# RWKV attention with a Fourier-mixing MLP block: six input tiles and four sets of chunk tiles in place of seven and three, with a new stored order

## The chip, the cores and the metric

The kernel runs on one core of a Trainium2 chip. The core has a matrix engine (PE, whose weight loads PEld overlap its matmuls), a vector engine (DVE), a scalar engine (ACT), GpSimd (POOL) and a queue engine (SP) that here only starts transfers between the chip's main memory (HBM) and the on-chip memory (SBUF). PE writes to eight banks of a second memory, PSUM. The metric is the device time of one execution in microseconds (us).

## The reference

Attention is a recurrence over 768 steps for 4 batches and 8 heads of 48 columns, with r, k, v and w of shape (4, 8, 768, 48) and u of shape (8, 48); its output, with the heads side by side, is x of shape (4, 768, 384). Behind it stand a two-dimensional Fourier transform of which the real part is kept, a layer norm, and an MLP with 1536 hidden columns:

```
def _attn_ref(r, k, v, w, u):
...
    for t in range(S):
...
        cur = np.einsum('bhd,bhe->bhde', u[None] * kt, vt)
        y[:, :, t] = np.einsum('bhd,bhde->bhe', rt, state + cur)
        state = wt[:, :, :, None] * state + np.einsum('bhd,bhe->bhde', kt, vt)
    return y.astype(np.float32)

def _moe_ref(x, w_ch1, w_ch2):
    X = np.fft.fft(x, axis=1)
    X = np.fft.fft(X, axis=2)
    mixed = np.real(X).astype(np.float32)
    u = x + mixed
...
    un = (u - mu) / np.sqrt(var + 1e-06)
    ch = np.maximum(un @ w_ch1, 0.0) @ w_ch2
    return (u + ch).astype(np.float32)
```

## The kernel before

**Attention in chunks.** Each batch is cut into six chunks of 128 steps, n = 0 to 23 in all. A chunk's four inputs (w, k, r, v, each 128 steps by 384 columns, fp32, 192 KB) are loaded by `load_one` (line 624) into one of NIN = 7 tiles of each kind, number n mod 7. `attention` (from line 783) takes the logarithm of w (LB, line 797), sums it over the steps on PE with a triangular mask (799, and 822 for the sum from the other side), and takes exponentials: those for r in place in PSUM or in the tile of w (852, 859), those for k in E2 with the chunk's whole decay (826, 836 to 840). RH is r times the first, KH is k times E2; the two stand side by side in RKH. Both are transposed into RKT, either by PE with a copy out of PSUM (893 to 911; the copies show at line 601 on ACT and 602 on DVE), or from batch 1 on by one DMA started by SP (889). The scores of KT and RT (922) are masked into AH (932 on DVE; or copied by ACT at 937 and masked in SBUF). The term with u is a dot product for each head: RK = r k, then RK times UB (u spread over all partitions, 660), then a sum over the head (DC, 871), and VTD = v DC. The state ST is carried from chunk to chunk (956, 959, 967), y is ST with RT plus AH with VB (984, 987; VB is v in bf16), and X = y + VTD (998). E2, RK, DC, AH and LB have NB = 3 tiles, number n mod 3; RKH and RKT have NT = 4. PE's sum for chunk n waits until the masks of chunk n - 2 are done.

**Mixing and MLP.** When chunks c and c + 3 of a batch are there, `fold` makes sums and differences of them (SD, XF). `mix` (from line 1048) does both transforms as matmuls (1063 to 1068, HCS, HCR, 1107), adds x (UF), normalises (UN), transposes in two halves of three tiles of 128 rows (UNT: by PE at 1203, or by a DMA of SP at 1210), multiplies by W1 (1235; HT is the rectified result, evicted by DVE at 1241 or by ACT at 1243) and W2 (1254), and evicts with the residual (OSB, 1263), which SP stores (1274). Elementwise work on SBUF tiles that either DVE or POOL can do shows at the helper lines 578 to 602. POOL's queue also starts the three loads of the weights (769, 774). PE does 32 filler matmuls (1321) that nothing reads.

**What sets the order.** All this is written down as numbered operations: `op` records one, and `choose` records several ways to do a step. The table `ORDER` lists for each engine the numbers in the order in which it runs them; a way whose numbers aren't in the table isn't taken. `schedule` only derives the PSUM banks from it by a model of times, and lets an operation of POOL on two SBUF tiles wait for the last such operation of DVE that the model puts ahead of it. `emit` gives each engine its list with the waits that the data need. An engine never overtakes within its list; SP, too, issues its transfers in the order of its list.

Of the kernel before, what the change touches and what calls it, by code (L numbers as in the profile page):

```python
# [7 lines left out]
ALU = mybir.AluOpType  # L8
# [442 lines left out]
def bass_rwkv6_finch__then__fnet_fourier_mix_kernel(  # L451
# [27 lines left out]
    def sb(name, shape, dt):  # L479
        return nc.alloc_sbuf_tensor(name, [128] + list(shape), dt).ap()  # L480

    NIN = 7
    NB = 3
    NT = 4
    INB = {n: [sb("in_%s%d" % (n, i), [H, D], FP32) for i in range(NIN)] for n in "wkrv"}
# [869 lines left out]
```

## Time and profile before

| what | us |
|---|---|
| median of 3 runs (lowest, highest) | 182.34 (182.21, 183.43) |
| the profiled execution: its own time | 182.32 |
| the profiled execution: its span | 180.2 |
| PE busy | 172.6 (96%) |
| DVE busy | 155.7 (86%) |
| ACT busy | 130.2 (72%) |
| POOL busy | 111.0 (62%) |

The span is what the profiler shows from the first to the last instruction; the rest of the execution's time lies around it. Matmuls are pipelined and their ends are modelled, so a busy PE is not PE at its peak. The granted clock of PE is at full speed in all slices. The 16 DMA engines together move 29.29 MB. Where the trace says that an engine waited "<- DMA in_w", the load of w into the tile ended the wait; "SPq" is an issue on SP's queue, and its length is the time that the issue held up the queue.

### The profile page before, as it was taken

The numbers are of one execution on the slowest core, as the hardware profiler recorded it, in microseconds if no ns is written. First come the engines' busy times: TensorE is split into PE (matmuls) and PEld (weight loads), VectorE is DVE, ScalarE is ACT, GpSimd is POOL, SyncE is SP. The second block draws the span as 40 slices with busy tenths as digits, with TensorE's granted clock in tenths as the row PEclk, the third lists the DMA queues.
The fourth block names the chain that finished last, engine by engine and source line by source line (L and its number), as shares of the span: only waits on it lengthen the run. The fifth ranks groups of instructions, "written<-read, shape, count | busy, mean of one in ns | idle before, by whom it ended". The sixth has DMA issues, their size and how long they took to land.

```text
span 180.2 us, 4569 instructions
## 1 busy us (share of the span) xinstructions
PE 172.6 (96%) x1704; PEld 113.9 (63%) x1704; DVE 155.7 (86%) x372; ACT 130.2 (72%) x311; POOL 111.0 (62%) x140
## 2 busy tenths in 40 slices
PE   5988899999999999999999999999999999999994
PEld 2455566766666576866676766665666776656663
DVE  7699999779998899999999999799999966882543
ACT  3989979589899686899997994986981754290500
POOL 2437779697464588599899865898988070310000
PEclk9999999999999999999999999999999999999999
DMA  5999998998998989999899999999973213304113
GB/s 118 209 209 204 178 200 169 183 208 163 171 206 173 211 166 241 202 204 210 191 216 187 232 161 210 233 160 196 217 162 51 91 44 63 135 4 100 39 58 131
DMA packets 117303, 29.29 MB, mean 163 GB/s; under 512 B 112545, under 2 KB 117282, under 8 KB 117282
## 3 DMA queue, kind: packets, MB, share of 16 engines
q1 hardware_dynamic: 115698, 26.65, 73.5%
q0 software_dynamic: 1584, 2.36, 7.7%
q8 instruction: 13, 0.21, 0.5%
q14 instruction: 8, 0.07, 0.1%
HBM read 23.59 MB, written 4.72 MB: 157 GB/s over the span
## 4 chain that ended last, share of the span: by engine, by line
PE 78%; DVE 7%; DMA 5%; ACT 4%; SPq 2%; issue 2%; POOL 1%; DVEq 0%; POOLq 0%; ACTq 0%
PE bank L1254 23%; PE bank L1235 23%; PE bank L1107 4%; PE bank L922 3%; PE bank L1063 3%; DMA in_v<-in_v_dram 3%; PE bank L911 3%; PE bank L1321 2%; PE bank L987 2%; DMA in_w<-in_w_dram 2%; PE bank L799 2%; PE bank L984 2%; PE bank L959 2%; SPq L889 1%; DVE ah L932 1%
## 5 line engine op out<-in xcount | busy, mean ns | idle before, releaser
L1254 PE MATMUL bank<-w,ht 128*128 128x384 bf16 (+2 forms) x300 | 52.8, 319 | 0.0
L1235 PE MATMUL bank<-unt,w 128*128 128x384 bf16 x288 | 52.0, 326 | 0.0
L1243 ACT ACTIVATE ht<-bank 128x384 bf16<-128x384 f32 x70 | 31.2, 497 | 13.2 <-PE bank L1235 13.0
L1254 PEld LDWEIGHTS bank<-w,ht 128*128 128x128 bf16 x300 | 27.5, 98 | 15.4
L1235 PEld LDWEIGHTS bank<-unt,w 128*128 128x128 bf16 x288 | 27.0, 98 | 15.7 <-DVE ah L932 0.2
L932 DVE TENSOR_TENSOR ah<-bank,msk 128x512 bf16<-128x512 f32 x42 | 27.4, 682 | 0.2 <-PE bank L922 0.2
L578 POOL TENSOR_TENSOR rkh<-in_k,e 128x384 bf16<-128x384 f32 x19 | 19.0, 1002 | 7.2 <-ACT e L840 4.9
L1263 DVE SCALAR_TENSOR_TENSOR osb<-bank,rstd,uf 128x384 f32<-128x384 f32 (+2 forms) x25 | 14.7, 596 | 9.0 <-PE bank L1254 9.0
L578 POOL TENSOR_TENSOR vtd<-in_v,dc 128x384 f32<-128x384 f32 x22 | 18.1, 830 | 5.7 <-DVE rk L578 4.1
L578 POOL TENSOR_TENSOR rk<-in_r,in_k 128x384 f32<-128x384 f32 x18 | 17.9, 1001 | 0.0
L578 POOL TENSOR_TENSOR rk<-rk,ub 128x384 f32<-128x384 f32 x17 | 16.9, 997 | 0.8 <-DVE rk L578 0.5
L1241 DVE TENSOR_SCALAR ht<-bank 128x384 bf16<-128x384 f32 x26 | 13.7, 547 | 2.9 <-PE bank L1235 2.9
L601 ACT ACTIVATE rkt<-bank 128x512 bf16<-128x512 bf16 (+1 forms) x19 | 14.5, 781 | 1.1 <-PE bank L911 1.1
L592 ACT ACTIVATE lb<-in_w 128x384 bf16<-128x384 f32 x24 | 12.3, 521 | 3.0 <-DMA in_w<-in_w_dram 2.9
L592 ACT ACTIVATE vb<-in_v 128x384 bf16<-128x384 f32 x23 | 11.9, 522 | 2.2 <-DMA in_v<-in_v_dram 2.2
L578 POOL TENSOR_TENSOR xf<-sd 128x384 bf16<-128x384 f32 (+1 forms) x9 | 8.9, 999 | 7.4 <-DVE xf L578 5.0
L871 DVE TENSOR_REDUCE dc<-rk 128x8 f32<-128x384 f32 (+1 forms) x24 | 12.5, 526 | 0.1
L853 DVE TENSOR_TENSOR rkh<-bank,in_r 128x384 bf16<-128x384 f32 x21 | 11.5, 547 | 0.4 <-ACT bank L852 0.4
L998 DVE TENSOR_TENSOR x<-bank,vtd 128x384 f32<-128x384 f32 x21 | 11.4, 549 | 0.2 <-POOL vtd L578 0.2
L826 ACT ACTIVATE e<-bank 128x392 f32<-128x392 f32 (+1 forms) x18 | 8.8, 497 | 3.4 <-PE bank L813 2.6
L852 ACT ACTIVATE bank<-bank 128x384 f32<-128x384 f32 x21 | 10.1, 486 | 1.7 <-PE bank L799 1.6
L987 PE MATMUL bank<-vb,ah 128*128 128x48 bf16 x192 | 11.1, 183 | 0.0
(185 smaller groups left out, 373.2 us busy)
## 6 DMA issues: line engine op xcount, KB each, us to landing
in_w<-in_w_dram SPq DMA_DIRECT2D x24, 192.0 KB, 3.8
in_r<-in_r_dram SPq DMA_DIRECT2D x24, 192.0 KB, 3.8
in_k<-in_k_dram SPq DMA_DIRECT2D x24, 192.0 KB, 3.9
in_v<-in_v_dram SPq DMA_DIRECT2D x24, 192.0 KB, 4.0
out_dram<-osb SPq DMA_DIRECT2D x23, 192.0 KB, 2.8
w<-in_moe_w_ch_dram POOLq DMA_DIRECT2D x2, 576.0 KB, 8.6
w<-in_moe_w_ch_dram POOLq DMA_DIRECT2D x1, 1152.0 KB, 11.1
out_dram<-osb SPq DMA_DIRECT2D x1, 128.0 KB, 1.7
```

Source lines behind the costliest of these rows:

```text
L578: return lambda e: e.tensor_tensor(out=o, in0=a, in1=b, op=f)
L592: return lambda e: e.activation(o, a, f, **kw)
L601: {"act": lambda e: e.activation(o(), i(), ACTF.Copy), "dve": lambda e: e.tensor_copy(out=o(), in_=i())}, **kw)
L853: op("dve", v_1(DM), lambda e: e.tensor_tensor(out=rh[:, :, 0:D], in0=ps(tce)[:, 0:DM].rearrange("t (h d) -> t h d", d=D), in1=rt[:, :, :] ...
L871: op("dve", v_1(H * m), lambda e: e.tensor_reduce(out=dc[:, :], in_=rku[:, :, 0:m], axis=mybir.AxisListType.X, op=ALU.add), r=[("RK", i2)] ...
L932: masked[n].append(op("dve", v_1(512), lambda e: e.tensor_tensor(out=ah[:, x:H:2, :], in0=ps(bk)[:, :].rearrange("p (h t) -> p h t", t=128 ...
L987: ins = e.matmul(ps(ty)[:, D * h:D * h + D], ah[:, h, :], vb[:, h, :], start=first and not ype, stop=True, skip_group_check=True)
L1235: ins = e.matmul(ps(t)[:, 0:384], W1[:, m, 256 * (j // 2) + j % 2:256 * (j // 2) + 256:2], unt[:, :, m, :], start=(m == 0), stop=(m == NM ...
L1241: {"dve": lambda e, j=j, t=t, ht=ht: e.tensor_scalar(out=ht[:, j, :], in0=ps(t)[:, 0:384], scalar1=su, scalar2=0.0, op0=ALU.mult, op1=ALU. ...
L1243: "act": lambda e, j=j, t=t, ht=ht: e.activation(ht[:, j, :], ps(t)[:, 0:384], ACTF.Relu, scale=su)},
L1254: ins = e.matmul(ps(t)[:, 0:hi - lo], ht[:, j, 128 * x:128 * x + 128], W2[:, j, lo:hi], start=(j == 0), stop=(j == NJ - 1))
L1263: op("dve", v_1(hi - lo) + 64, lambda e: e.scalar_tensor_tensor(out=o[:, lo:hi], in0=ps(t)[:, 0:hi - lo], scalar=rstd[:, kb:kb + 1], in1=u ...
```

## The change

The input tiles go from seven to six of each kind, and E2, RK, DC and AH from three to four; LB stays at three. The product RK times UB moves from the common path into the way `dots`. A further way `dots_pe` is written for batch 0, which would do the dot product on PE; the new table doesn't take it. What it needs is made all the same in `bonus`: a pattern HV by POOL, UBD from it by two instructions of DVE, three small fp32 matmuls on PE (`spread`) and one product of DVE; nothing reads the result. And the table `ORDER` is new as a whole.

```
-    NIN = 7
-    NB = 3
+    NIN = 6
+    NB = 4
     NT = 4
...
-    LB = [sb("lb%d" % i, [H, 64], BF16) for i in range(NB)]
+    LB = [sb("lb%d" % i, [H, 64], BF16) for i in range(3)]
...
+        op("pool", 120, lambda e: e.iota(HV[:, :, :], [[128, NM], [-D, H]], base=0, channel_multiplier=1,
+                                         allow_small_or_imprecise_dtypes=True), w=["HV", ("UNT", 0, 2)])
+        op("dve", 80, ts(UBD[:, :, :], HV[:, :, :], -0.5, None, ALU.is_gt), r=["HV", ("UNT", 0, 2)], w=["UBD"])
+        op("dve", 90, stt(UBD[:, :, :], HV[:, :, :], D - 0.5, UBD[:, :, :], ALU.is_lt, ALU.mult), r=["HV", ("UNT", 0, 2)], w=["UBD"])
+        th = g.tile("f")
+
+        def spread(e):
+            for m in range(NM):
+                ins = e.matmul(ps(th)[:, H * m:H * m + H], UR[0:1, 128 * m:128 * m + 128], ONF[0:1, 0:H], start=True,
+                               stop=True, skip_group_check=True)
+            return ins
+        op("pe", 560, spread, r=["ONF", "UR"], w=[th])
+        op("dve", 95, lambda e: e.tensor_tensor(
+            out=UBD[:, :, :], in0=ps(th)[:, 0:NM * H].rearrange("p (m h) -> p m h", h=H), in1=UBD[:, :, :], op=ALU.mult),
+           r=[th, ("UNT", 0, 2)], w=["UBD"])
...
-        L = LB[i2]
+        L = LB[n % 3]
...
-        vec(DM, tt(rku[:, :, :], rk[:, :, :], UB[:, :, :], ALU.mult),
-            r=[("RK", i2), "UB"], w=[("RK", i2)])
 
         def dots(m):
+            vec(DM, tt(rku[:, :, :], rk[:, :, :], UB[:, :, :], ALU.mult), r=[("RK", i2), "UB"], w=[("RK", i2)])
...
-        g.choose(("dots", b, c), lambda: dots(D), lambda: dots(D // 2))
+        g.choose(("dots", b, c), lambda: dots(D), lambda: dots(D // 2), *([dots_pe] if b == 0 else []))
```

The lines of the changed kernel have other numbers: 578 is 582 there, 624 is 628, 889 is 928, 1210 is 1249, 1274 is 1313, and so on. Three places of the new order follow, the lists of an engine before and now; a number in a name is that of the tile.

SP late in the program, before: `rkh2` and `rkh3` belong to chunks 0 and 1 of batch 3, `rkh1` and `rkh0` to its chunks 3 and 2; `in_w6` is the w of chunk 2 and `in_v0` the v of chunk 3.

```order
L624 DMA in_w1<-in_w_dram 128x8x48
L889 DMA_TRANSPOSE rkt2<-rkh2 128x8x128
L889 DMA_TRANSPOSE rkt3<-rkh3 128x8x128
L624 DMA in_r6<-in_r_dram 128x8x48
L1274 DMA out_0_dram<-osb0 128x384
L624 DMA in_w6<-in_w_dram 128x8x48
```

```order
L1274 DMA out_0_dram<-osb2 128x384
L624 DMA in_w2<-in_w_dram 128x8x48
L889 DMA_TRANSPOSE rkt1<-rkh1 128x8x128
L889 DMA_TRANSPOSE rkt0<-rkh0 128x8x128
L624 DMA in_v0<-in_v_dram 128x8x48
```

Now, where the same two loads go to `in_w2` and `in_v3`:

```order
L628 DMA in_w2<-in_w_dram 128x8x48
L628 DMA in_w4<-in_w_dram 128x8x48
L628 DMA in_v1<-in_v_dram 128x8x48
L928 DMA_TRANSPOSE rkt2<-rkh2 128x8x128
L928 DMA_TRANSPOSE rkt3<-rkh3 128x8x128
L628 DMA in_k3<-in_k_dram 128x8x48
```

```order
L628 DMA in_v3<-in_v_dram 128x8x48
L628 DMA in_v2<-in_v_dram 128x8x48
L1313 DMA out_0_dram<-osb1 128x384
L928 DMA_TRANSPOSE rkt1<-rkh1 128x8x128
L928 DMA_TRANSPOSE rkt0<-rkh0 128x8x128
```

The w of chunk 2 went from behind the first pair of transposes to ahead of it, and the v of chunk 3 from behind the second pair to ahead of it; other loads of batch 3 went back.

DVE near the start, around the first products with UB, before:

```order
L578 TENSOR_TENSOR rk0<-in_r0,in_k0 128x384
L589 MEMSET ss 128x3
L589 MEMSET rkh1 128x8x8
L589 MEMSET rkh0 128x8x8
L589 MEMSET cs 128x3
L578 TENSOR_TENSOR rk0<-rk0,ub 128x384
L578 TENSOR_TENSOR rk1<-in_r1,in_k1 128x384
L578 TENSOR_TENSOR rk1<-rk1,ub 128x384
```

and now:

```order
L593 MEMSET rkh1 128x8x8
L593 MEMSET ss 128x3
L593 MEMSET cs 128x3
L582 TENSOR_TENSOR rk1<-in_r1,in_k1 128x384
L582 TENSOR_TENSOR rk0<-rk0,ub 128x384
L582 TENSOR_TENSOR rk1<-rk1,ub 128x384
L873 TENSOR_TENSOR rkh1<-bank3,in_r1 128x8x48
```

The product of r and k of chunk 0 went to POOL, and that of chunk 1 from behind the first product with UB to ahead of it.

DVE while batch 1's attention runs beside batch 0's MLP, up to the fourth result that it evicts; `ah1` before and `ah2` now are the masked scores of the same chunk, 4 of batch 1. Before, where the eviction is entry 148 of the list:

```order
L967 TENSOR_TENSOR bank2<-bank2,e2_0 128x384
L998 TENSOR_TENSOR x1<-bank3,vtd1 128x384
L853 TENSOR_TENSOR rkh3<-bank1,in_r4 128x8x48
L578 TENSOR_TENSOR sd<-x1 128x385 x2
L932 TENSOR_TENSOR ah1<-bank4,msk 128x4x128
L932 TENSOR_TENSOR ah1<-bank3,msk 128x4x128
L967 TENSOR_TENSOR st0<-bank2,e2_1 128x384
L1263 SCALAR_TENSOR_TENSOR osb2<-bank5,rstd0,uf0 128x384
L998 TENSOR_TENSOR x1<-bank3,vtd2 128x384
```

and now, where it is entry 155:

```order
L1037 TENSOR_TENSOR x1<-bank2,vtd1 128x384
L873 TENSOR_TENSOR rkh3<-bank3,in_r5 128x8x48
L593 MEMSET mco 128x1
L1006 TENSOR_TENSOR bank1<-bank1,e2_1 128x384
L582 TENSOR_TENSOR sd<-x1 128x385 x2
L971 TENSOR_TENSOR ah2<-bank3,msk 128x4x128
L971 TENSOR_TENSOR ah2<-bank5,msk 128x4x128
L1006 TENSOR_TENSOR st0<-bank1,e2_2 128x384
L1302 SCALAR_TENSOR_TENSOR osb2<-bank6,rstd0,uf0 128x384
L1037 TENSOR_TENSOR x1<-bank3,vtd2 128x384
```

The rows around it are nearly the same, but seven more entries stand ahead of the eviction.

More of the change, by code (lines that the diff above doesn't have):

```diff
@@ L873, in dots, with dots_pe, turn, dot @@
                r=[("RK", i2)], w=[("DC", i2)])
-        g.choose(("dots", b, c), lambda: dots(D), lambda: dots(D // 2))
+        def dots_pe():
+            t = g.tile("a")
+            row = rk[:, :, :].rearrange("t h d -> t (h d)")
+            def turn(e):
+                for m in range(NM):
+                    ins = e.matmul(ps(t)[:, 128 * m:128 * m + 128], row[:, 128 * m:128 * m + 128], IDF[:, :], start=True,
+                                   stop=True, skip_group_check=True)
+                return ins
+            def dot(e):
+                for m in range(NM):
+                    ins = e.matmul(ps(t)[:, DM:DM + H], row[:, 128 * m:128 * m + 128], UBD[:, m, :], start=m == 0,
+                                   stop=m == NM - 1, skip_group_check=True)
+                return ins
+            op("pe", 1100, turn, r=["IDF", ("HT", 0, 0), ("RK", i2)], w=[t])
+            evict(lambda: row, lambda: ps(t)[:, 0:DM], DM, r=[t], w=[("RK", i2)])
+            op("pe", 560, dot, r=[("RK", i2), "UBD", ("UNT", 0, 2)], w=[t])
+            evict(lambda: dc[:, :], lambda: ps(t)[:, DM:DM + H], H, more=20, r=[t], w=[("DC", i2)])
+        g.choose(("dots", b, c), lambda: dots(D), lambda: dots(D // 2), *([dots_pe] if b == 0 else []))
         op(None, {"pool": 787, "dve": v_1(DM)}, tt(vtd[:, :, :], vt[:, :, :],
```

14 lines of the change are left out of this document (8 added, 6 removed), and 138 rows, old and new, of the table ORDER.

## The prediction

> **What bounds the kernel now.** I read the page first, then a table by stretch, then the chain of waits with the waits by engine, and last single stretches of the trace. All sums go against the profiled execution: 182.32 us, of which 180.2 are the span and 2.1 lie around it. The median of the three runs, 182.34, is in effect the same. The page, then the table (length of the stretch, then busy us and instructions of each engine, granted clock, DMA share, GB/s):
>
> ```profile
> span 180.2 us, 4569 instructions
> PE 172.6 (96%) x1704; PEld 113.9 (63%) x1704; DVE 155.7 (86%) x372; ACT 130.2 (72%) x311; POOL 111.0 (62%) x140
> ```
>
> ```profile
> 0.00:10.00 10.00, 8.10 (x43) 3.92 (x43) 7.50 (x38) 6.65 (x11) 3.24 (x14) 1.00 0.87 171
> 10.00:30.00 20.00, 17.95 (x232) 11.76 (x232) 19.77 (x42) 17.39 (x36) 14.69 (x20) 1.00 0.98 192
> 30.00:48.00 18.00, 17.99 (x184) 12.62 (x183) 15.38 (x41) 14.63 (x35) 13.72 (x18) 1.00 1.02 178
> 48.00:62.00 14.00, 14.00 (x138) 8.96 (x136) 12.62 (x28) 12.17 (x33) 7.15 (x10) 1.00 1.04 194
> 62.00:100.00 38.00, 38.00 (x455) 26.54 (x454) 37.58 (x83) 33.70 (x80) 32.94 (x37) 1.00 1.00 203
> 100.00:125.00 25.00, 23.95 (x255) 15.90 (x253) 23.43 (x52) 20.65 (x53) 20.17 (x22) 1.00 1.09 198
> 125.00:144.00 19.00, 19.00 (x184) 12.81 (x183) 18.58 (x43) 12.71 (x34) 13.04 (x15) 1.00 0.65 136
> ```
>
> PE is gap-free from 30 us on except for 1.05 us between 100 and 125 (25.00 less 23.95). Its other holes, 1.90 and 2.05 us, lie in the first 30 us, where PE waits for the start-up chain and then for DVE (19.77 of 20.00 busy). So time can be gained in three ways only: start sooner, lose the 1.05 us, or give PE less work. DVE is the second bound: 37.58 of 38.00 between 62 and 100. Its spare time lies ahead of that, 2.62 us in 30 to 48 and 1.38 in 48 to 62. At the end PE runs without a hole, as the chain of waits shows:
>
> ```profile
> 165.89 5.85 PE bank L1235 x36
> 171.74 5.89 PE bank L1254 x48
> ```
>
> 36 matmuls of 384 columns take 5.85 us, 162.5 ns each; the change adds none and removes none of these, and 32 fillers stand in both orders.
>
> **The start.** What PE's first real work waits for, from the chain of waits, and what DVE does behind it, from the time line:
>
> ```profile
> 0.97 0.42 POOL osb L636
> 1.39 0.28 POOL osb L634
> ...
> 4.60 0.37 DVE ht L582
> ...
> 5.22 0.79 ACT cs L592
> 6.02 1.29 ACT L709
> ...
> 8.34 0.39 ACT ub L601
> ```
>
> ```profile
> 8.82 0.56 DVE L578 TENSOR_TENSOR rk<-rk,ub 128x384 f32<-128x384 f32 x1 [1.42 <-ACT ub L601]
> 9.29 0.55 DVE L578 TENSOR_TENSOR rk<-in_r,in_k 128x384 f32<-128x384 f32 x1
> ```
>
> DVE sits idle for 1.42 us until ACT has written UB, and then multiplies r and k of chunk 1. The new order puts that product ahead of UB's, into the idle time: 0.55 us off a DVE that is otherwise full there (its in_r1 and in_k1 now stand 7th and 2nd in SP's queue, before 6th and 7th). Against this the sine arguments move: POOL makes the two ramps in the other order, takes one of DVE's three roundings, and DVE does two small fills and a mask earlier. Walking both lists with these durations I get the second sine (5.22) 0.1 to 0.2 us later and with it the table load at 6.02. Sum for the start: -0.3 us; bounds -0.6 (the product saved and no delay) and +0.4 (the delay, and the first chunk-2 loads, which land about two places later, awaited).
>
> **The spread matmuls and UBD.** Their result feeds nothing, since the alternative that reads it isn't taken. Three fp32 matmuls of 8 columns are not in the trace. Nearest rows: the fp32 UB matmul with its 384 columns, and the 2-column totals.
>
> ```profile
> L660 PE MATMUL bank<-osb,vtd x2: 481/533/585, 7.3 to 7.7; 1*128 1x384 f32 x2
> L813 PE MATMUL bank<-one,lb 128*128 128x2 bf16 x80 | 4.7, 163 | 0.0
> ```
>
> They bound the three between nothing (the totals' 163 ns overlap their neighbours almost wholly) and 3 x 0.53 us. I take 0.2, near the small ones, as these have 8 columns. They stand ahead of the UB matmul, whose second half ends at about 8.2 (7.7 and 0.48), while ACT is free for UB's copy only at 8.34, behind both logarithms: that hides 0.15, and +0.1 stays on the path, 0 to +1.4. DVE's three UBD operations come later and are in its count below.
>
> **The two DMA waits.** PE's holes between 100 and 125 both end with a late load, by the waits of PE (the last two rows; the first belongs to the start) and the chain:
>
> ```profile
> PE bank L922 <- ACT rkt L601: 0.9, 2, 0.5
> PE bank L799 <- ACT lb L592: 0.7, 1, 0.7
> ...
> PE bank L959 <- ACT st L601: 0.3, 1, 0.3
> ```
>
> ```profile
> 105.20 2.17 SPq L889
> ...
> 108.06 0.63 SPq L1274
> 108.73 3.62 DMA in_w<-in_w_dram
> 112.38 0.53 ACT lb L592
> ...
> 117.65 0.49 SPq L889
> 118.20 4.62 DMA in_v<-in_v_dram
> 122.84 0.53 ACT vb L592
> ```
>
> SP works its list in order. The w of chunk 2 of batch 3 is issued only after the two transposes of rkh at L889, which wait for DVE's rows; the v of chunk 3 likewise behind the next pair. In the new order both stand ahead of their pair: w at least 3.5 us sooner (108.73 less 105.20), v at least 0.55 (118.20 less 117.65), each more than the hole it made (0.7 and 0.3). That takes the whole 1.05 us: -1.05, with 0 as the other end, if some other operand arrives as late. Loads that moved back are the v of chunks 0 and 1 of batch 3 (SP places 82 to 86 and 81 to 90). The later one was issued at 93.22 (row below); nine places of about 1 us and 4.6 us of flight make 107, by ACT's list about when it casts it.
>
> **Six input tiles.** A load now waits for the chunk six before it, not seven. The nearest margin is that of v, batch 3, chunk 1, whose tile is freed by the second product of this row and whose issue stands in the next:
>
> ```profile
> 88.42 2.42 POOL L578 TENSOR_TENSOR vtd<-in_v,dc 128x384 f32<-128x384 f32 x3
> ```
>
> ```profile
> 93.22 0.90 SPq L624 DMA_DIRECT2D in_v<-in_v_dram  x1
> ```
>
> It was free at about 90.0 (88.42 and two thirds of 2.42) and issued at 93.2, and now stands nine places later. Other loads have more room. Cost: 0. What hides it is that SP issues loads as fast as the DMA queues take them (share 0.98 to 1.09 of the 16 engines up to 125 us). The fourth set of E2, RK, DC and AH only removes write-after-read waits, and no row here shows PE waiting for one; I take 0.
>
> **DVE in the middle.** Total DVE work is alike, but it is dealt out earlier. Up to the fourth result eviction (list entry 148 before, 155 now), whose matmuls stand at the same place in PE's work within 0.2 us, DVE has more to do. By rows:
>
> ```profile
> L932 DVE TENSOR_TENSOR ah<-bank,msk 128x512 bf16<-128x512 f32 x42 | 27.4, 682 | 0.2 <-PE bank L922 0.2
> L1241 DVE TENSOR_SCALAR ht<-bank 128x384 bf16<-128x384 f32 x26 | 13.7, 547 | 2.9 <-PE bank L1235 2.9
> L998 DVE TENSOR_TENSOR x<-bank,vtd 128x384 f32<-128x384 f32 x21 | 11.4, 549 | 0.2 <-POOL vtd L578 0.2
> L583 DVE TENSOR_SCALAR un<-uf,agg 128x384 bf16<-128x384 f32 x3 | 1.2, 409 | 0.0
> ```
>
> Two more score masks (ACT had them, 2 x 0.68), one more HT (0.55), one UN (0.41), half a cosine table (0.43), UBD (about 0.5) and a score transpose (about 0.4), less one of UB's products, one x and one state (each 0.55) and a table negation (0.4): about +1.8 us. DVE's 4.0 us of spare time between 30 and 62 can hold this, if its inputs come sooner there, and they do: in the new order PE produces them about 2 us of its work earlier relative to DVE. If all fits, nothing is lost; if none, PE pays 1.8. I take +0.5, because PE and DVE run without spare time for 80 us after that, so a few short waits are likelier than none.
>
> **The tail.** The last transpose of UN by DMA hangs on DVE's last UN, which now has about 1.2 us more DVE work ahead, while PE's use stands 0.5 us earlier. DVE is far from full there (from 144 us on: 6.64 of 10 by the row below, PE full), so I take +0.1, with 0 to +0.5.
>
> ```profile
> 144.00:154.00 10.00, 10.00 (x73) 6.66 (x72) 6.64 (x21) 4.93 (x16) 3.81 (x6) 1.00 0.21 49
> ```
>
> **Sum.** 182.3 - 0.3 + 0.1 - 1.05 + 0.5 + 0.1 = 181.65, so 181.7 us.
>
> **The rivals.** *DVE keeps its idle time* (slower). If DVE still waits about 4 us between 30 and 62, it enters the full stretch 1.8 us late, and by the eleventh eviction the new order asks another 0.2 to 1.5 us more of it. DVE is then the bound up to 144 us and the loads no longer matter, so the 1.05 us is not saved: 182.3 - 0.3 + 2.0 to 3.3, about 184.6. It decides from some 2 us of idle that remain there; each further us costs up to one. For it: 37.58 of 38.00 leaves no way to catch up. Against: most of that idle time was a wait for PE, which is now ahead.
>
> *Nothing is given back* (faster). The start gives its -0.6, both late holes close, half of PE's 0.9 us behind ACT's copies of transposes goes too (DVE now makes two of the first copies), and middle and tail cost nothing: 182.3 - 0.6 - 0.45 - 1.05 = 180.2. For it: DVE's spare time is twice what is needed. Against: DVE at the start has no spare time to make those copies in.
>
> *The holes move* (same). The two loads come earlier, others later, and PE waits as long for v of chunk 1 or for a transpose: 182.3 - 0.3 + 0.3 = 182.3.
>
> *DVE and POOL block each other* (slower). These rows, of DVE's products and of one that met a POOL product:
>
> ```profile
> L578 DVE TENSOR_TENSOR rk<-in_r,in_k x6: 535/569/1383, 6.7 to 57.1; 128x384 f32<-128x384 f32 x6
> ```
>
> ```profile
> 57.07 1.00 POOL L578 TENSOR_TENSOR rk<-in_r,in_k 128x384 f32<-128x384 f32 x1
> ```
>
> The sixth took 1.38 us where the others take 0.55: it lasts until POOL's is over. Each new meeting on the full stretch costs DVE up to 0.8 us. The number of DVE operations that read two SBUF tiles is 50 before and 51 now, so on average nothing changes; three unlucky meetings would give 181.7 + 2.4, about 184.1. The Trainium skill, page "SBUF — State Buffer", section "Who interferes with whom", says that a DVE instruction with two SBUF inputs and a GpSimd one that reads SBUF exclude each other, the second waiting for the first to end. The row of 1.38 us agrees with this; that the median of the six is 0.57 says that meetings are rare. By the rule applied to three of the new order's meetings the sum is the 184.1 above, by the median row it stays 181.7.
>
> **How the numbers follow.** About 1%, 1.8 us, is what a measurement of this kernel tells from no change; the bounds are 180.5 and 184.2. Chances: forecast 0.45 (own range 180.5 to 183.3, a tenth of it below 180.5), nothing given back 0.21 (nine tenths of it below 180.5), DVE keeps its idle time 0.20 (most above 184.2), the holes move 0.09, blocking 0.05 (half above). Faster: 0.045 + 0.19, about 0.23. Slower: 0.17 + 0.03 and some for what I don't see, 0.23. Same: 0.54. The range runs from 179.9 (start and late holes at their best ends, and 0.7 of PE's waits at the start) to 184.6.
>
> **What would show it.** Right: no gap of PE between 100 and 125; DVE's product of r and k of chunk 1 inside the wait for UB; DVE busier from 30 to 62 than the 28.0 us of now, by 1.8 or so. Wrong: PE waits for DVE's masks or evictions between 62 and 100 (rival one); DVE's products at 1.0 us or more in numbers (blocking); a PE wait behind ACT's cast of v near 107 (holes moved); a wait for UNT near 165 (tail).

## The result, and the profile after

The changed kernel took 184.76 us (median of 3 runs, 184.41 to 185.72) where the kernel before took 182.34: a ratio of 1.0129, 95% interval [1.0088, 1.017]. Two repeats of the unchanged code beside the experiments gave 1.0107 [1.0067, 1.0148] and 1.0069 [1.0045, 1.0093]. So the change costs 0.7 to 1.3%, about 1.3 to 2.4 us, where 0.6 us less was forecast. The time lies just above the range, which ended at 184.6; the medians of the two repeats, 183.95 and 183.85, lie inside it. Medians hold all executions, while ratios leave out the few that lie more than 1.5% above the fastest of their kernel.

The profiled execution of the changed kernel was the slowest of the three, 185.72 us. Its page, and its table by stretch with the columns of the one before:

```profile
span 183.6 us, 4582 instructions
...
PE 174.0 (95%) x1710; PEld 115.1 (63%) x1710; DVE 157.3 (86%) x376; ACT 131.6 (72%) x317; POOL 110.1 (60%) x139
```

```profile
0.00:10.00 10.00, 8.69 (x46) 4.65 (x46) 7.32 (x37) 6.29 (x9) 3.85 (x16) 1.00 0.82 161
10.00:30.00 20.00, 17.27 (x225) 11.60 (x225) 19.04 (x40) 16.98 (x37) 15.92 (x22) 1.00 1.00 196
30.00:48.00 18.00, 18.00 (x193) 12.42 (x191) 16.25 (x47) 15.64 (x38) 11.71 (x15) 1.00 1.03 187
48.00:62.00 14.00, 13.44 (x127) 8.42 (x124) 12.79 (x27) 9.85 (x27) 4.20 (x6) 1.00 0.97 173
62.00:100.00 38.00, 37.83 (x452) 26.47 (x451) 37.09 (x82) 33.21 (x78) 33.19 (x36) 1.00 0.98 202
100.00:125.00 25.00, 23.77 (x249) 15.93 (x248) 24.35 (x56) 20.53 (x54) 20.39 (x23) 1.00 1.16 181
```

In the changed kernel L961 is the scores (922 before), L1274 the product with W1 (1235), L1293 that with W2 (1254), L1302 the eviction of results (1263) and L819 the sum over the steps (799); edits shift these numbers by up to three. The waits of PE that are new behind 30 us (total, times, longest), and the chain of waits around the two long ones:

```profile
PE bank L961 <- DMA rkt<-rkh: 1.2, 1, 1.2
PE bank L1274 <- DMA unt<-un: 1.1, 1, 1.1
...
PE bank L1293 <- DMA w<-in_moe_w_ch_dram: 0.6, 1, 0.6
```

```profile
118.80 5.23 DMA rkt<-rkh
124.17 0.62 PE bank L961 x16
...
163.71 4.75 DMA unt<-un
168.51 5.05 PE bank L1274 x30
```

The waits for w and for v between 100 and 125 are gone. In that stretch PE now waits 1.2 us for a transpose of chunk rows; elsewhere it waits 1.1 us for the last transpose of UN and, between 48 and 62, 0.6 us for W2. One execution of three can hold chance events, so here is the repeat's profile too, of an execution of 183.12 us (0.8 below its own median). Two stretches of it, and its waits of PE:

```profile
62.00:100.00 38.00, 37.82 (x448) 26.44 (x446) 37.08 (x83) 33.39 (x79) 33.29 (x37) 1.00 0.98 200
100.00:125.00 25.00, 24.47 (x260) 16.41 (x259) 24.62 (x57) 20.75 (x55) 20.27 (x22) 1.00 1.01 182
```

```profile
PE bank L961 <- DVE osb L1302: 0.5, 1, 0.5
PE bank L1274 <- DMA unt<-un: 0.4, 1, 0.4
...
PE bank L819 <- DVE ah L971: 0.2, 1, 0.2
```

The wait for W2 is gone, and that at L961 is now 0.5 us behind DVE's result eviction (L1302), which frees the bank that the scores are to be written to. DVE is busy 24.62 of 25.00 us there. Of 15 profiles in the new order, with and without further edits, 12 have that wait behind DVE (0.2 to 0.5 us; in the other three a transpose of chunk rows came later still) and all have the wait for the last UNT (0.2 to 1.1 us); of the five in the old order none has the one or the other. These two belong to the order; the wait for W2 to one execution.

The start, first DVE's product of chunk 1, then the first work of PE behind the fillers, then ACT's table load, logarithms and UB copy:

```profile
8.82 0.56 DVE L582 TENSOR_TENSOR rk<-in_r,in_k 128x384 f32<-128x384 f32 x1 [1.57 <-DMA in_r<-in_r_dram]
9.29 1.02 DVE L582 TENSOR_TENSOR rk<-rk,ub 128x384 f32<-128x384 f32 x2
```

```profile
7.07 0.83 PE L675 MATMUL bank<-vtd,osb 1*128 1x8 f32 x6
7.76 0.89 PE L664 MATMUL bank<-osb,vtd 1*128 1x384 f32 x2
```

```profile
6.35 1.28 ACT L729 ACT_TABLE_LOAD   x1
7.74 0.94 ACT L596 ACTIVATE lb<-in_w 128x384 bf16<-128x384 f32 x2
8.69 0.49 ACT L605 ACTIVATE ub<-bank 128x384 f32<-128x384 f32 x1
```

The product stands ahead of UB's, as the new order says, but it waits 1.57 us for in_r1 where DVE waited 1.42 for UB: the two starts, 8.82 and 9.29, are those of before in the other order. The spread matmuls take 0.69 us (7.07 to 7.76; each of the three shows as two). The table load is 0.33 later than before (6.35 against 6.02), UB's copy 0.45 (8.69 against 8.24 on ACT's time line). In the first 30 us PE stands still for 4.04 us in this profile and for 3.56 in the repeat, where it was 3.95 before, and it has the 0.69 us of spread matmuls more to do: the start is no shorter.

### The profile page after: what moved, and what is told of

Read it like the earlier page. It is cut to its first block, busy times and chain, and to the rows that moved or that the text cites. A ratio compares the mean times of both kernels' runs of the same rounds, so it can differ in the third digit from the quotient of the medians.

```text
span 183.6 us, 4582 instructions
## 1 busy us (share of the span) xinstructions
PE 174.0 (95%) x1710; PEld 115.1 (63%) x1710; DVE 157.3 (86%) x376; ACT 131.6 (72%) x317; POOL 110.1 (60%) x139
## 4 chain that ended last, share of the span: by engine, by line
PE 56%; DVE 16%; DMA 15%; issue 4%; POOL 4%; SPq 2%; ACT 1%; POOLq 0%; DVEq 0%
PE bank L1293 18%; PE bank L1274 14%; DMA w<-in_moe_w_ch_dram 7%; PE bank L1146 4%; DMA rkt<-rkh 3%; DMA unt<-un 3%; PE bank L961 2%; DVE ah L971 2%; PE bank L1102 2%; DMA in_r<-in_r_dram 2%; DVE rk L582 2%; SPq L628 2%; PE bank L950 2%; PE bank L1360 2%; PE bank L1026 2%
## 5 line engine op out<-in xcount | busy, mean ns | idle before, releaser
L1293 PE MATMUL bank<-w,ht 128*128 128x384 bf16 (+2 forms) x300 | 53.0, 319 | 0.6 <-DMA w<-in_moe_w_ch_dram 0.6
L1274 PE MATMUL bank<-unt,w 128*128 128x384 bf16 x288 | 52.0, 326 | 1.1 <-DMA unt<-un 1.1
L1293 PEld LDWEIGHTS bank<-w,ht 128*128 128x128 bf16 x300 | 27.6, 98 | 16.2 <-DMA w<-in_moe_w_ch_dram 0.7
L1274 PEld LDWEIGHTS bank<-unt,w 128*128 128x128 bf16 x288 | 26.8, 98 | 17.4 <-DMA unt<-un 1.5
L971 DVE TENSOR_TENSOR ah<-bank,msk 128x512 bf16<-128x512 f32 x44 | 28.7, 679 | 0.8 <-PE bank L961 0.5
L582 POOL TENSOR_TENSOR vtd<-in_v,dc 128x384 f32<-128x384 f32 x24 | 19.8, 834 | 6.4 <-DVE rk L582 3.3
L582 POOL TENSOR_TENSOR rk<-rk,ub 128x384 f32<-128x384 f32 x18 | 17.9, 1006 | 5.1 <-DVE rk L582 4.9
L1302 DVE SCALAR_TENSOR_TENSOR osb<-bank,rstd,uf 128x384 f32<-128x384 f32 (+2 forms) x24 | 14.1, 593 | 7.9 <-PE bank L1293 7.6
L1280 DVE TENSOR_SCALAR ht<-bank 128x384 bf16<-128x384 f32 x28 | 15.0, 548 | 5.6 <-PE bank L1274 5.5
L582 POOL TENSOR_TENSOR rk<-in_r,in_k 128x384 f32<-128x384 f32 x17 | 17.0, 1008 | 2.2 <-DVE rk L582 1.5
L582 POOL TENSOR_TENSOR xf<-sd 128x382 bf16<-128x382 f32 (+1 forms) x11 | 11.0, 1005 | 7.1 <-DVE pe L586 2.9
L596 ACT ACTIVATE vb<-in_v 128x384 bf16<-128x384 f32 x22 | 11.3, 518 | 1.2 <-DMA in_v<-in_v_dram 1.2
L873 DVE TENSOR_TENSOR rkh<-bank,in_r 128x384 bf16<-128x384 f32 x20 | 11.0, 550 | 1.2 <-ACT bank L872 0.9
L1037 DVE TENSOR_TENSOR x<-bank,vtd 128x384 f32<-128x384 f32 x20 | 10.8, 546 | 0.2
```

The costliest lines, as they stand in the source:

```text
L582: return lambda e: e.tensor_tensor(out=o, in0=a, in1=b, op=f)
L596: return lambda e: e.activation(o, a, f, **kw)
L873: op("dve", v_1(DM), lambda e: e.tensor_tensor(out=rh[:, :, 0:D], in0=ps(tce)[:, 0:DM].rearrange("t (h d) -> t h d", d=D), in1=rt[:, :, :] ...
L971: masked[n].append(op("dve", v_1(512), lambda e: e.tensor_tensor(out=ah[:, x:H:2, :], in0=ps(bk)[:, :].rearrange("p (h t) -> p h t", t=128 ...
L1274: ins = e.matmul(ps(t)[:, 0:384], W1[:, m, 256 * (j // 2) + j % 2:256 * (j // 2) + 256:2], unt[:, :, m, :], start=(m == 0), stop=(m == NM ...
L1280: {"dve": lambda e, j=j, t=t, ht=ht: e.tensor_scalar(out=ht[:, j, :], in0=ps(t)[:, 0:384], scalar1=su, scalar2=0.0, op0=ALU.mult, op1=ALU. ...
```

## The experiments

Each stands beside runs of the kernel before on the same chip (medians 182.21 to 182.47 us); the ratio is to those.

### Tiles and sets alone

The kernel before, its order untouched:

```
-    NIN = 7
-    NB = 3
+    NIN = 6
+    NB = 4
...
-    LB = [sb("lb%d" % i, [H, 64], BF16) for i in range(NB)]
+    LB = [sb("lb%d" % i, [H, 64], BF16) for i in range(3)]
...
-        L = LB[i2]
+        L = LB[n % 3]
```

> The kernel before, old order, with six input tiles of each kind and four sets of E2, RK, DC and AH (LB at three). Forecast's step: no load waits for a tile and no write waits for a set, so 182.1 to 182.6. Rival 'tiles': loads wait for their tiles (margin of 3.2 us for the v of chunk 1 of batch 3, with all else early or late by less), 183 or more.

Measured 182.39 us, 0.9995 [0.9968, 1.0021]. Six tiles and four sets cost nothing and bring nothing in the old order.

### The two loads alone, each way

SP's list of the kernel before, with the two loads ahead of their pairs:

```
+L624 DMA in_w6<-in_w_dram 128x8x48
 L889 DMA_TRANSPOSE rkt2<-rkh2 128x8x128
 L889 DMA_TRANSPOSE rkt3<-rkh3 128x8x128
...
-L624 DMA in_w6<-in_w_dram 128x8x48
...
+L624 DMA in_v0<-in_v_dram 128x8x48
 L889 DMA_TRANSPOSE rkt1<-rkh1 128x8x128
 L889 DMA_TRANSPOSE rkt0<-rkh0 128x8x128
-L624 DMA in_v0<-in_v_dram 128x8x48
```

> The kernel before with two loads moved: the w of chunk 2 of batch 3 ahead of the first pair of rkh transposes, the v of chunk 3 ahead of the second, as in the new order; nothing else. Forecast's step: PE's two waits go, 1.05 us, 181.4. Theory 'waits are traded': a load ahead of a transpose makes the transpose land later by what the load takes, and PE waits for that instead: the w load was not behind a tight transpose, so 0.3 to 0.8 us are gained, 181.7 to 182.1, and a wait for RKT appears near 121 us.

Measured 181.42 us, 0.9954 [0.9922, 0.9986], 0.9 us less than before. It is the fastest kernel of this study. The stretch and its waits:

```profile
100.00:125.00 25.00, 24.70 (x269) 16.50 (x266) 24.30 (x53) 21.16 (x54) 20.67 (x22) 1.00 1.10 204
```

```profile
PE bank L923 <- DMA rkt<-rkh: 0.3, 1, 0.3
```

Of the 1.05 us of holes 0.30 are left, behind a transpose. Now the reverse in the new order, for v alone: the v of chunks 2 and 3 go behind the second pair, and the w stays ahead.

```
-L628 DMA in_v3<-in_v_dram 128x8x48
-L628 DMA in_v2<-in_v_dram 128x8x48
...
 L928 DMA_TRANSPOSE rkt1<-rkh1 128x8x128
 L928 DMA_TRANSPOSE rkt0<-rkh0 128x8x128
+L628 DMA in_v3<-in_v_dram 128x8x48
+L628 DMA in_v2<-in_v_dram 128x8x48
```

> The changed kernel with the v of chunks 2 and 3 of batch 3 put behind the second pair of rkh transposes, where the kernel before had one of them. Theory 'waits are traded': the transposes land 0.5 to 1 us sooner (flight 3.5 to 4.5 in place of 4.2 to 5.9), the wait of 0.6 to 1.4 us near 122 us gets smaller or moves to the cast of v, and the time stays within 0.4 us of the changed kernel. If the loads ahead of the transposes are what costs: 0.5 to 1.0 faster, 183.2. If they are a gain: 0.4 to 0.5 slower.

Measured 185.3 us, 1.0158 [1.0118, 1.0197], where the repeats of the changed kernel stand at 1.0107 and 1.0069. The chain shows the late load, and the waits what it holds up:

```profile
120.34 3.63 DMA in_v<-in_v_dram
...
124.00 0.52 ACT vb L596
124.52 0.38 ACT st L605
```

```profile
PE bank L998 <- ACT st L605: 0.8, 1, 0.8
```

The moved loads are a gain in the old order, and that of v in the new one too; what they give is spent elsewhere there.

### The start and the unused preparation, a first look

The changed kernel again; then without the preparation (pattern, UBD, spread, product; nothing reads its result); then with the start's tables as before; then with both edits.

> The changed kernel, unaltered, for a second profile. Theory 'start and transposes' (PE is behind by about 1.0 us when it reaches 30 us, and then loses three waits for transfers, 0.7 for W2, 1.4 for a transpose of rkh at 124 us and 1.2 for the last transpose of un at 168 us): about 184.6; the start and the two middle waits come again, the last one may be smaller, since in the first profile that transpose took 4.75 us and the execution, 185.72 us, was 1 us above the median. Rival 'DVE is the bound' (DVE's 1.8 us of extra work before the fourth eviction sets the pace): about 184.6 too, but the waits of PE lie behind DVE between 62 and 144 us.

Measured 183.95 us, 1.0107 [1.0067, 1.0148].

```
-        op("pool", 120, lambda e: e.iota(HV[:, :, :], [[128, NM], [-D, H]], base=0, channel_multiplier=1,
+        def unused():
+            op("pool", 120, lambda e: e.iota(HV[:, :, :], [[128, NM], [-D, H]], base=0, channel_multiplier=1,
...
+        g.choose("spread", lambda: None, unused)
```

> The changed kernel without the preparation that nothing reads (HV, UBD, the three small fp32 matmuls, the product). Theory 'start and transposes': the three small matmuls hold the UB matmul up by 0.7 us, but ACT isn't free for UB's copy before the logarithms end, so 0.1 to 0.4 us faster than the changed kernel, 184.2 to 184.5. Rival 'DVE is the bound': 0.4 faster by DVE's three small operations, 184.2. If the matmuls were costless: 184.6.

Measured 182.72 us, 1.0004 [0.9975, 1.0032]: no slower than before.

The third has POOL's two ramps in their old order, the rounding back on DVE and POOL's fill of XF back at its later place.

> The changed kernel with the sine tables' start as before: POOL makes the ramps in the old order and fills XF later, and DVE rounds all three rows. Theory 'start and transposes': the table load on ACT comes 0.3 us sooner, but UB still waits for the small matmuls: 0 to 0.2 us faster than the changed kernel, 184.4 to 184.6. Rival 'DVE is the bound': one more DVE operation, 184.6 to 184.9.

Measured 183.58 us, 1.0071 [1.0044, 1.0099]. The table load came only 0.12 us earlier.

> Both edits of the start together. Theory 'start and transposes': UB is ready 0.4 to 0.7 us sooner, and PE reaches its first 30 us of work that much sooner: 183.9 to 184.2, if the later waits for transfers do not eat it. Rival 'DVE is the bound': the same gain at the start, since DVE starts sooner too, 184.0; so this run tells how much the start is worth and not which of the two holds later.

Measured 183.54 us, 1.0073 [1.0048, 1.0099], no better than the tables alone. So the effects don't add: leaving the preparation out gains 1.0% with the new tables and nothing with the old ones. Why isn't shown.

### The last transpose of UN

SP issues it at the same time in the kernel before and in the repeat of the changed one:

```profile
161.99 1.55 SPq L1210 DMA_TRANSPOSE unt<-un  x1
```

```profile
161.79 1.28 SPq L1249 DMA_TRANSPOSE unt<-un  x1
```

Before, it landed 3.19 us after that, and PE didn't wait. In the repeat it took 4.06, in the first profile 4.75. The page lists 13 packets of 16 KB on the queue of instruction fetches, in both kernels alike:

```profile
q8 instruction: 13, 0.21, 0.5%
```

One of them falls near this transpose. Packet times from the trace, in us: the fetch's start against the issue, the longest time of any of the transpose's 1,184 packets, and its flight from issue to landing.

```
kernel                              fetch    longest packet   flight
before                              +0.11        0.15          3.19
before, loads ahead                 -0.19        0.21          3.19
before, six and four                -0.13        0.36          3.09
changed                             +1.49        2.03          4.75
changed, repeat                     +1.10        1.35          4.06
changed, tables as before           +0.99        1.53          4.23
changed, no preparation             +1.17        1.87          4.60
changed, v loads behind             +1.02        1.13          3.84
```

The transpose's first packet starts 1.17 to 1.19 us after the issue. In the five profiles of the old order the fetch, which takes 1.0 to 1.7 us, is over by then to within 0.04 us, and no packet is held up. In all 15 of the new order it begins 1.0 to 1.9 us after the issue and runs beside the packets until 2.1 to 2.9, and the flight is 3.84 to 4.75. Two other transposes bear on this. The one of UN before the last has no fetch near it, and in the same 15 profiles it flies 2.83 to 2.86 us, so the new order doesn't slow every transpose. The one of chunk rows issued near 130 us flies 3.33 to 3.89 us in these 15, where a fetch is still under way when its packets start, and 2.77 to 3.15 in the five of the old order, which have none there. The theory that the two collide was tried by moving the fetch: more instructions of PE ahead of it (14 wide and 14 narrow early fillers in place of 16 wide ones), with and without the preparation, or fewer in the kernel before (9 fillers of 512 columns in place of 16 of 384); then narrow matmuls at the program's end.

```
-        for i in range(NE):
+        for i in range(14):
             ins = e.matmul(ps(tw)[:, 0:384], W1[:, 0, 0:128], W1[:, 0, 0:384])
+        for i in range(14):
+            ins = e.matmul(ps(tw)[:, 0:8], W1[:, 0, 0:128], W1[:, 0, 0:8])
```

> The changed kernel with 14 wide and 14 narrow (8-column) matmuls in PE's first, idle block in place of 16 wide ones: 24 more PE instructions, about the same time there. Theory 'fetch': in the changed kernel a 16 KB instruction fetch of PE falls 1.1 to 1.5 us behind the issue of the last transpose of un, into its packets, and holds them up (flight 4.1 to 4.8 us, PE waits 0.6 to 1.2); with 24 instructions more ahead of it the fetch comes some 2 us sooner, before the packets. Flight about 2.8 to 3.2, PE's wait below 0.2, and 0.6 to 1.1 us faster than the changed kernel: about 183.1. Rival 'the transpose is slow for another reason' (its place in the queue, its tiles): the wait stays, about 184.0.

Measured 184.28 us, 1.013 [1.0083, 1.0178]; flight 3.88.

> The same 24 instructions and no preparation that nothing reads. Theory 'fetch' and 'start' together: 0.6 to 1.1 us faster than without the preparation alone (182.72), so 181.6 to 182.1, at or under the kernel before. Rival 'the transpose is slow for another reason': 182.7.

Measured 182.76 us, 1.0028 [0.9993, 1.0062]; flight 4.36.

> The kernel before with 9 matmuls of 512 columns in PE's first, idle block in place of 16 of 384: 14 PE instructions fewer. Theory 'fetch': its fetch moves from 0.1 us behind the issue of the last transpose of un to about 1.2 behind it, into the packets; flight 4 us or more in place of 3.2, PE waits 0.5 to 1.2, and it is that much slower than before: 182.9 to 183.5. Rival 'another reason': 182.4.

Measured 182.91 us, 1.0019 [0.9988, 1.005]; flight of the last transpose 3.20. But in this profile a fetch fell into an earlier transpose of UN (issued at 119.87), which flew 5.01 us where it takes 3.5 to 4.2 in the other profiles of the old order. PE waited 1.1 us at the product with W1 that reads it; but the trace puts the end of that wait to an operation of DVE that ended 0.03 us after the landing, so the transpose alone isn't shown to be its cause.

The last two add 12 narrow matmuls to the end of the changed kernel, and 6 to the end of the kernel before.

> The changed kernel with 12 narrow matmuls (24 PE instructions) behind its last useful one, under the last store. The earlier 24 at the front did not move the fetch against the program (205 instructions stood behind it in both), so its place seems to be counted from the end. Theory 'fetch': it now comes about 2 us later, behind the transpose's packets; flight 2.8 to 3.3 us, PE's wait before the last W1 stage below 0.2, 0.5 to 0.9 us faster than the changed kernel, 183.2 or so. If the place is not counted from the end, the fetch stays 1.1 to 1.5 us behind the issue and nothing changes (184.0). Rival 'the transpose is slow for another reason': the fetch moves and the flight stays above 4.

Measured 183.9 us, 1.0073 [1.0045, 1.0102]; flight 4.33.

> The kernel before with 6 such matmuls (12 instructions) at the end. Theory 'fetch': the fetch comes about 1 us behind the last transpose's issue, into its packets; flight 4 us, PE waits 0.4 to 0.8 near 165 us, 182.7 to 183.1. Rival 'another reason': 182.3 and flight 3.2.

Measured 182.2 us, 0.9993 [0.9968, 1.0019]; flight 3.20.

In none of the five did the fetch move against the last transpose: it starts 0.2 to 0.3 us ahead of the issue in the old order's two and 1.0 to 1.1 behind it in the new one's three. These runs were to tell the collision from some other cause, and did not. That a fetch beside the packets and a long flight go together is what 20 profiles show; that the one causes the other isn't shown by an edit that moves the fetch alone. The Trainium skill, page "Runtime: NRT & Kernel Launch", section "Instruction fetch mechanics", says that each engine's sequencer fetches its program in blocks of 16 KiB by a DMA queue of its own and that the cost of crossing a block is mostly hidden. The size agrees with the packets here. The page speaks of the engine that fetches, not of a transfer beside the fetch; if the one here does hold up the transpose, the 0.6 to 1.6 us aren't hidden.

### The unused preparation, taken apart

Why should it cost over 1 us? Three candidates: the matmuls on PE ahead of UB, DVE's three operations, and the PSUM bank held from the matmuls near 7 us to DVE's product at 35 to 40. The changed kernel and the one without the preparation ran beside the first two edits on the same chip, the last two edits on another.

> The changed kernel unedited, as the base for the three runs beside it. Both theories: about 184 us, 0.8 to 1.3% above the kernel before.

Measured 183.85 us, 1.0069 [1.0045, 1.0093].

> The changed kernel without the unused preparation, a repeat beside the other three. Both theories: 1.0 to 1.4 us less than the unedited kernel beside it.

Measured 182.67 us, 1.0014 [0.999, 1.0037].

Only the matmuls kept (pattern, UBD and product not taken):

```
+        g.choose("pattern", lambda: None, unused)
...
+        g.choose("product", lambda: None, product)
```

> The changed kernel with the three spread matmuls kept where they are, but without the pattern, without DVE's three operations and without the product, so that the bank that the matmuls write is free at once. Theory one (the cost of the unused preparation lies in the matmuls ahead of UB's, 0.69 us of PE on the path to UB): no gain, within 0.3 us of the unedited kernel beside it. Theory two (it lies in the bank that is held from about 7 us until DVE's product near 35 us, or in DVE's operations): about 1.2 us less, at the kernel without the preparation.

Measured 183.06 us, 1.0033 [1.0012, 1.0053].

All kept, and the matmuls moved on PE:

```
-L675 MATMUL bank<-vtd,osb 128x8 x3
 L664 MATMUL bank<-osb,vtd 128x384
...
+L675 MATMUL bank<-vtd,osb 128x8 x3
 L938 MATMUL bank<-idw,rkh 128x128 x8
```

> The changed kernel with everything kept, but with the three spread matmuls moved from ahead of UB's matmul to the place at about 11.6 us where PE waits 0.66 us for POOL's KH. Theory one (matmuls ahead of UB's): about 1.2 us less than the unedited kernel, and UB's copy by ACT some 0.3 to 0.6 us earlier. Theory two (bank or DVE): no gain, within 0.3 us, as the bank is still held from about 12 us to 35 and DVE's list is the same.

Measured 184.42 us, 1.0098 [1.0066, 1.013]. UB's copy came at 8.59 (9.35 in the unedited kernel beside it, 8.87 in the earlier repeat), and it gained nothing. With the matmuls alone in their old place the copy came at 8.59 too. So it isn't the place ahead of UB.

All kept, but DVE's product takes HV in place of the matmuls' result, so that the bank is free at once:

```
-            out=UBD[:, :, :], in0=ps(th)[:, 0:NM * H].rearrange("p (m h) -> p m h", h=H), in1=UBD[:, :, :], op=ALU.mult),
+            out=UBD[:, :, :], in0=HV[:, :, :], in1=UBD[:, :, :], op=ALU.mult),
```

> The changed kernel with the whole unused preparation in its places, except that DVE's product takes HV from SBUF in place of the result of the spread matmuls (which nothing reads in either), so that the PSUM bank is free at once and not near 35 us. If the held bank is the cost: near the kernel with the matmuls alone, 0.3% above the kernel before, about 183.1 us. If DVE's three operations (about 0.5 us of DVE ahead of its full stretch) are the cost: no gain, 0.7 to 1.0% above the kernel before, about 183.9 us.

Measured 183.63 us, 1.0075 [1.0046, 1.0104]: no gain seen from the bank. The edit isn't quite clean, as the product takes 0.46 us from SBUF where it takes 0.18 from the bank.

The same with the matmuls left out (`g.choose("matmuls", lambda: None, matmuls)`):

> The changed kernel without the three spread matmuls, but with POOL's pattern and DVE's three operations in their places, the last on SBUF tiles alone. If the held bank (or the matmuls) is the cost: near the kernel without the preparation, 0.0 to 0.2% above the kernel before, about 182.6 us. If DVE's operations are: 0.5 to 0.8% above the kernel before, 183.3 to 183.7 us, and PE's short wait for DVE's masks near 73 us is there, as in the kernels with the preparation.

Measured 183.08 us, 1.0046 [1.002, 1.0072].

Side by side: DVE's operations cost 0.0036 of the time with the matmuls there (1.0069 less 1.0033) and 0.0032 without (1.0046 less 1.0014), about 0.6 us; the matmuls 0.0023 and 0.0019, about 0.4 us. Each single difference has a half width of about 0.003, so DVE's part rests on both pairs agreeing, and the matmuls' part is no more than likely.

A rival stands beside the first pair. `schedule` derives the PSUM banks anew from each list, and with the bank no longer held to 35 us, 62 to 64 of the 319 results that PE puts in a bank follow another one there than in the changed kernel. Among the four kernels without the held bank (nothing kept, the matmuls, DVE's part, all with the bank freed) at most 6 do. These four agree with the pairs above: DVE's part, with the slower product, costs 0.0032 without the matmuls and 0.0042 (1.0075 less 1.0033) with them, the matmuls 0.0019 and 0.0029. So DVE's part doesn't hang on the order of the banks; POOL's pattern goes with it in every run and wasn't parted from it.

Some of DVE's part can be seen as a wait of PE in the kernel with DVE's part alone, 0.2 us of the 0.6:

```profile
PE bank L822 <- DVE ah L974: 0.2, 1, 0.2
```

It is the sum of a later chunk at about 72 us, behind DVE's masks, which start 0.3 us later here than in the kernel without the preparation (70.83 against 70.51). Nine of the ten profiles with DVE's three operations have a wait of 0.2 us or more for the masks between 62 and 100, and none of the five in the new order without them. Where the other 0.4 us go isn't shown. Something else shows in the stretch from 10 to 30 us, here of the kernel with the bank freed early and then of that without the matmuls:

```profile
10.00:30.00 20.00, 17.70 (x221) 12.22 (x221) 18.41 (x39) 16.45 (x36) 15.40 (x22) 0.91 0.99 195
```

```profile
10.00:30.00 20.00, 17.56 (x239) 12.12 (x239) 19.26 (x41) 17.59 (x39) 16.53 (x23) 1.00 1.01 198
```

The granted clock is 0.91 in the first. The time line of PE in the two, at the same instructions:

```profile
10.14 0.78 PE L773 MATMUL bank<-cs,idw 1*128 1x191 bf16 x6
10.76 0.48 PE L773 MATMUL bank<-ss,unt 128*128 128x193 bf16 x2
...
14.34 0.40 PE L961 MATMUL bank<-rkt 48*128 48x128 bf16 x8
```

```profile
10.14 0.78 PE L776 MATMUL bank<-cs,idw 1*128 1x191 bf16 x6
10.76 0.33 PE L776 MATMUL bank<-ss,unt 128*128 128x193 bf16 x2
...
13.36 0.40 PE L964 MATMUL bank<-rkt 48*128 48x128 bf16 x8
```

Up to 10.76 us they agree to the hundredth; then the first runs slower, and its first scores start 0.98 us later (14.34 against 13.36). Single microseconds of the changed kernel that ran beside them:

```profile
10.00:11.00 1.00, 1.00 (x15) 0.59 (x13) 1.00 (x3) 1.00 (x3) 0.00 (x0) 0.84 1.07 217
11.00:12.00 1.00, 1.00 (x6) 0.68 (x6) 1.00 (x3) 1.00 (x4) 0.89 (x2) 0.50 0.95 185
...
13.00:14.00 1.00, 1.00 (x13) 1.00 (x11) 0.75 (x3) 0.57 (x2) 0.00 (x0) 0.50 1.05 204
14.00:15.00 1.00, 1.00 (x21) 0.82 (x19) 0.69 (x2) 1.00 (x3) 0.54 (x1) 0.95 1.22 245
```

At half clock for 0.32 + 3 + 0.10 = 3.42 us. Such a dip, of 3.42 us each time by the same sum, stands in 4 of the 9 profiles of kernels with the whole preparation in the new order, and in none of the other 11. But a profile is one execution. Half of 3.42 us is 0.9% of 182, so an execution with one dip has a mean granted clock of 0.99, and the record of all executions shows this mark (0.989 to 0.991) elsewhere too: in 14 of 59 of these kernels, in 4 of 66 of the others in the new order, in 10 of 116 of the kernel before, beside which the experiments ran, and in 3 of 48 of its edits, all three with the 9 fillers. So the preparation isn't needed for a dip; dips come more often with it (24% against 7%). And they aren't its price: without the marked executions the medians of the changed kernel and of the one without the preparation beside it are 183.74 and 182.63, still 1.1 us apart. The Trainium skill, page "TensorE: Matmul & The Clock Gate", section "Part 1: The HAM clock gate (the "warmup" mystery)", says that the clock is either half or full, set by how busy the array was in windows of about 3.4 us that run freely and don't start with the kernel. The 3.42 us and the 0.50 agree, and so does that only some executions have the dip.

## Why the prediction was wrong, point by point

**The two DMA waits (-1.05): right in the mechanism, half given back.** Alone, the moved loads gave 0.9 us in the old order, and their undoing for v cost 0.5 to 0.9% in the new. In the new order both waits are gone. The saving was confirmed by an edit, so it wasn't luck. What the forecast named as the other end, that "some other operand arrives as late", came in part: 0.5 us behind DVE's result eviction in that stretch.

**Six tiles, fourth set (0): right,** as far as the old order shows it.

**The start (-0.3): wrong sign.** This step failed: "puts that product ahead of UB's, into the idle time: 0.55 us off a DVE". It took in_r1's place in SP's queue, 7th where it was 6th, for harmless; but in_r1 landed 1.3 to 1.8 us later (at 8.5 to 9.1 us against 7.25), when the wait was nearly over, and the product saved nothing. The table load slipped by 0.33 where 0.1 to 0.2 was taken. Without the preparation PE stands still for 4.09 us of the first 30 (10 less 8.47 and 20 less 17.44) where it was 3.95 before: about +0.1 in place of -0.3. Undoing the tables' part brought at most 0.4% and, without the preparation, made it slower; so what the tables' order is worth stays open.

**Spread and UBD (+0.1): the largest miss.** Leaving the preparation out gained 0.55%, 1.0% and 1.0% in three pairs of kernels, 1.0 to 1.9 us, and nothing in a fourth, with the old tables. This term failed by its size: work that nothing reads was priced at 0.1 on the way to UB, and its cost lies elsewhere. On PE the matmuls took 0.69 us, inside the bounds (0 to 1.6) but not the 0.2 taken from the row of the bf16 totals; these are fp32, and the fp32 UB row was the nearer one. DVE's three operations (0.53 us in the profile, counted under DVE's middle) cost about 0.6, in full, which fits that DVE has hardly any spare time behind 62 us (37.08 of 38.00 busy in the repeat). The half-clock dip, about 1 us in 14 of 59 executions, was in no term and no rival; but the kernel before has it too, in 10 of 116.

**DVE in the middle (+0.5): about right.** DVE's busy time from 30 to 62 us is 29.65 in the repeat (16.31 and 13.34) against 28.00, +1.65 of the 1.8 forecast, so it fits into the spare time. The items of the forecast's list add up to 1.6, not to its 1.8, which is nearer still. The short waits that were expected came: 0.2 behind a mask, which the kernels without DVE's three operations lack, and the 0.5 behind an eviction that is named above and counts once.

**The tail (+0.1): undersized.** The sign that was named, "a wait for UNT near 165", came, 0.2 to 1.1 us; but not because DVE's UN was late: SP issued the transpose at the same time. The transpose itself took 0.6 to 1.6 us longer; why is the open question above.

**The rivals.** DVE keeping its idle time gave 184.6, close to the result by luck: DVE filled 1.65 of the 4.0 us, and PE waits for it only 0.2 us between 62 and 100, so DVE isn't the bound there. DVE and POOL blocking each other wasn't needed: the products of r and k have a mean of 552 ns in the repeat and 616 in the first profile, where one of seven took 1.02 us; before, it was 718. (Of the row of 1.38 us the prediction says that it lasts until POOL's is over; it ends 0.4 us behind it, at 58.48 against 58.07.)

```profile
L582 DVE TENSOR_TENSOR rk<-in_r,in_k 128x384 f32<-128x384 f32 x7 | 3.9, 552 | 1.4 <-DMA in_r<-in_r_dram 1.4
```

Holes that move came nearest: -1.05, and back 0.5 at L961 and up to 1.0 at UNT. For the kernel without the preparation these alone give 182.3 - 1.05 + 0.5 + 1.0 = 182.75 with its profile's waits, and 182.67 was measured; its start comes out even. The preparation's 1.2 us on top, which is the difference measured, make the 183.85 beside it. The two waits, in the profile of the kernel without the preparation:

```profile
PE bank L1275 <- DMA unt<-un: 1.0, 1, 1.0
...
PE bank L962 <- DVE osb L1303: 0.5, 1, 0.5
```

Together: the forecast is 2.2 us short of that repeat. About 1.1 is the preparation, 0.4 the start, and 0.4 to 0.9 the last transpose (waits of 0.5 and 1.0 with and without the preparation, where 0.1 was taken); the 0.5 behind the eviction is what was taken for the middle. This sum is an estimate from waits and differences.

## What to carry to other kernels

Work whose result nothing reads isn't free: price it on each engine it touches, and take it in full where that engine has no spare time afterwards. When it is taken out to see what it costs, look at what else moves with it, such as the banks that are derived from the list. When an operation is moved into a wait, look up when its own inputs land in the new queue, not only whether the wait is long enough. And try the one move that the profile asks for alone: the two loads gave 0.9 us in the old order, while the new order around them lost it and 1.3 to 2.4 us more.

## What the runs showed of the hardware

- PE's granted clock fell to 0.50 for 3.42 us in 4 of 20 profiles, between 10 and 16 us. In the pair compared it cost 0.98 us. By the mean clock of each execution this happens to the kernel before too, in 10 of 116.
- A DMA transpose of 1,184 packets landed 3.1 to 3.2 us after its issue in 5 profiles where a 16-KB instruction fetch was over when its packets started, and after 3.8 to 4.75 us in 15 where the fetch ran beside them; single packets then took 1.1 to 2.0 us.
- Three fp32 matmuls of 8 columns and one row took 0.69 us on PE and show as six of 251 ns in the median.
